# Both MLP products by three one-pass products, with the weights' parts fetched from HBM, in place of the Strassen-Winograd scheme

## The chip, the cores and the metric

The kernel runs on one core of a Trainium2 chip. The metric is the device time of one execution in microseconds (us); all times below are us unless marked ns. The result section says how ratios are computed.

## The reference

```python
kv  = einsum('bhsd,bhse->bhde', k, v)            # q, k, v: 8 x 8 x 576 x 64, fp32
out = einsum('bhsd,bhde->bhse', q, kv)
x   = out / sqrt(mean(out*out, -1) + 1e-6) * g_norm   # -> 4608 tokens x 512
h   = x @ w_in                                   # 512 x 2048
g   = h * erf(softplus(h))
y   = g @ w_out                                  # 2048 x 512
```

## The kernel before

The 4608 tokens are nine groups of 512. Group 0 multiplies in plain fp32. Groups 1 to 8 use a Strassen-Winograd scheme: seven products of half blocks in place of eight, in fp32 (four passes of TensorE), with the block sums on VectorE. The weights stay in SBUF for the whole run. The hidden features of a group are worked through in four **batches** of four 128-feature tiles; beside each batch runs a quarter of the next group's attention (two heads).

```python
def product(a, x, ps=None, first=True, last=True):          # groups 1 to 8
    ...
    for i in range(2):
        for c in range(2):
            nc.tensor.matmul(ps[:, i * H : i * H + H],      # 256 columns, fp32
                lhsT=a[:, c, i * P : i * P + P], rhs=x[:, c, :], ...)
    return ps
# --- cut: the seven hidden and seven result products of a batch, with sums ---
w_in_sb = const.tile([P, KC, DF], FP32, name="w_in_sb")     # resident weights
w_out_sb = const.tile([P, FC, DM], FP32, name="w_out_sb")
# --- cut ---
def norm():                              # the end of a quarter's attention
    ms, u, r = (st.pop(name) for name in ("ms", "u", "r"))
    nc.vector.scalar_tensor_tensor(out=u, in0=ms, scalar=EPS, in1=u, ...)   # reads PSUM
    ...
```

## Time and profile before

The median before is 1028.89 (1027.05 to 1029.86); with the run beside the changed kernel 1029.12.

| before | value | how to read it |
|---|---|---|
| TensorE (PE) busy | 1000.5, 97% of the span | the bound |
| VectorE (DVE), ScalarE (ACT) busy | 712.7, 498.5 | beside it |
| one Strassen matmul, 256 columns, fp32 | 0.2158 spacing | 112 a batch make 24.17 |
| a batch with its attention | 27.36 | a quarter of the stretch of 109.44 |
| DMA engines' busy share in that stretch | 0.15 | transfers matter nowhere after the start |

The lines that these come from stand in the prediction.

### The profile page before, as it was taken

The page shows a single profiled execution, that of the slowest core. Times are in us where ns is not written, and L with a number is a line of the kernel's source. Part 1 is how long each engine was busy: PE and PEld are TensorE (multiplying, and loading weights), DVE is VectorE, ACT ScalarE, POOL GpSimd, SP SyncE. Part 2 cuts the span into 40 slices and gives each one's busy share as a digit, 9 for nine tenths or more (in the row PEclk, how much of TensorE's full clock was granted, in tenths as well). Part 3 has the DMA queues.
Part 4 walks back from the last instruction along what each step waited for, and adds up shares of the span by engine and source line. Part 5 has one row for each costly group of instructions (what it writes and reads, how often), then busy time and mean ns, then how long its engine had stood idle before and what let it go on. Part 6 is the DMA issues. An engine that isn't in the chain of part 4 may idle for free.

```text
span 1028.0 us, 12344 instructions
## 1 busy us (share of the span) xinstructions
PE 1000.5 (97%) x4968; PEld 805.8 (78%) x4968; DVE 712.7 (69%) x1169; ACT 498.5 (48%) x654; POOL 2.4 (0%) x10
## 2 busy tenths in 40 slices
PE   6779999999999999999999999999999999999997
PEld 3334446788888888888888888888888888888886
DVE  1887895788786667657766577667865786677555
ACT  2787773444454455454444444444545544442222
POOL 0000000000000000000000000000000000000000
PEclk9999999999999999999999999999999999999999
DMA  9755511211121112001121112111200010001001
GB/s 269 203 173 159 157 42 34 78 34 37 34 77 34 37 34 74 18 22 34 49 62 34 36 34 77 34 36 34 75 1 1 1 41 1 1 1 41 1 1 42
DMA packets 67337, 55.32 MB, mean 54 GB/s; under 512 B 39632, under 2 KB 61136, under 8 KB 67280
## 3 DMA queue, kind: packets, MB, share of 16 engines
q1 hardware_dynamic: 65392, 52.24, 17.1%
q10 hardware_dynamic: 1824, 2.29, 0.8%
q8 instruction: 39, 0.64, 0.3%
q14 instruction: 18, 0.15, 0.0%
q0 software_dynamic: 64, 0.00, 0.0%
HBM read 45.09 MB, written 9.44 MB: 53 GB/s over the span
## 4 chain that ended last, share of the span: by engine, by line
PE 91%; DVE 5%; ACT 2%; DMA 1%; issue 0%; DVEq 0%
PE p_ps L521 74%; PE o_ps L370 4%; PE h_ps L445 3%; PE se_ps L292 3%; PE kv_ps L270 2%; PE qt_ps L286 2%; DMA k_sb<-in_k_dram 1%; PE ms_ps L314 1%; PE ms_ps L313 1%; DVE w_m L211 1%; DVE w_e L207 1%; DVE e L469 1%; PE kv_ps L278 1%; PE kv_ps L291 0%; DVE w_in_sb L221 0%; DVE w_out_sb L221 0%
## 5 line engine op out<-in xcount | busy, mean ns | idle before, releaser
L469 DVE TENSOR_TENSOR h_sb<-h_sb,p_ps 128x512 f32<-128x512 f32 x224 | 150.6, 684 | 160.3 <-PE p_ps L521 159.5
L393 ACT ACTIVATE s_sb<-h_sb 128x512 f32<-128x512 f32 x144 | 90.7, 630 | 312.2 <-DVE h_sb L469 311.4
L521 PE MATMUL p_ps<-w_out_sb,h_sb 128*128 128x256 f32 x768 | 176.2, 379 | 0.0
L521 PEld LDWEIGHTS p_ps<-w_out_sb,h_sb 128*128 128x128 f32 x768 | 145.9, 190 | 19.9
L521 PE MATMUL p_ps<-x_sums,a_sums 128*128 128x256 f32 x512 | 120.9, 379 | 0.0
L521 PE MATMUL p_ps<-x_sums,w_in_sb 128*128 128x256 f32 x512 | 120.9, 379 | 0.0
L521 PE MATMUL p_ps<-w_sums,s_sb 128*128 128x256 f32 x512 | 120.8, 379 | 0.0
L521 PEld LDWEIGHTS p_ps<-x_sums,a_sums 128*128 128x128 f32 x512 | 97.3, 190 | 23.9 <-issue 12.0
L469 DVE TENSOR_TENSOR e<-e,p_ps 128x512 f32<-128x512 f32 x120 | 80.7, 684 | 43.4 <-PE p_ps L521 42.2
L521 PEld LDWEIGHTS p_ps<-x_sums,w_in_sb 128*128 128x128 f32 x512 | 97.1, 190 | 14.4
L521 PEld LDWEIGHTS p_ps<-w_sums,s_sb 128*128 128x128 f32 x512 | 97.3, 190 | 13.2
L521 PE MATMUL p_ps<-xT,w_in_sb 128*128 128x256 f32 x448 | 101.3, 379 | 0.0
L521 PEld LDWEIGHTS p_ps<-xT,w_in_sb 128*128 128x128 f32 x448 | 83.2, 190 | 10.3
L100 ACT ACT_TABLE_LOAD x69 | 88.5, 1283 | 1.2
L469 DVE TENSOR_TENSOR h_sb<-h_sb,s_sb 128x512 f32<-128x512 f32 x128 | 82.2, 684 | 2.0 <-ACT s_sb L398 2.0
L398 ACT ACTIVATE s_sb<-s_sb 128x512 f32<-128x512 f32 x144 | 78.8, 618 | 0.4
L295 ACT ACTIVATE qT<-se_ps 128x512 f32<-128x512 f32 x32 | 19.1, 596 | 122.2 <-PE se_ps L292 122.2
L445 PE MATMUL h_ps<-xT,w_in_sb 128*128 128x512 f32 x128 | 61.1, 623 | 5.2 <-DVE w_in_sb L221 5.2
L521 PE MATMUL p_ps<-w_out_sb,s_sb 128*128 128x256 f32 x256 | 60.5, 379 | 0.0
L521 PE MATMUL p_ps<-w_sums,h_sb 128*128 128x256 f32 x256 | 60.5, 379 | 0.0
L370 PE MATMUL o_ps<-w_out_sb,h_sb 128*128 128x512 f32 x128 | 57.5, 593 | 0.4 <-DVE h_sb L402 0.4
L521 PEld LDWEIGHTS p_ps<-w_out_sb,s_sb 128*128 128x128 f32 x256 | 48.6, 190 | 6.6
(89 smaller groups left out, 1121.4 us busy)
## 6 DMA issues: line engine op xcount, KB each, us to landing
k_sb<-in_k_dram SPq DMA_DIRECT2D x29, 288.0 KB, 4.2
v_sb<-in_v_dram SPq DMA_DIRECT2D x29, 288.0 KB, 4.1
q_sb<-in_q_dram SPq DMA_DIRECT2D x32, 256.0 KB, 3.3
w_raw<-in_moe_w_out_dram SPq DMA_DIRECT2D x8, 1024.0 KB, 4.8
w_raw<-in_moe_w_in_dram SPq DMA_DIRECT2D x7, 1024.0 KB, 5.6
out_dram<-e SPq DMA_DIRECT2D x28, 256.0 KB, 2.1
q_last<-in_q_dram SPq DMA_DIRECT2D x16, 64.0 KB, 4.6
w_raw<-in_moe_w_in_dram SPq DMA_DIRECT2D x2, 512.0 KB, 6.3
```

Of the source, the lines that this page charges most:

```text
L100: nc.scalar.preload_act_table_set("softplus")
L207: nc.vector.scalar_tensor_tensor(out=e, in0=hi, scalar=-(1 << 31), in1=e, op0=ALU.bitwise_and, op1=ALU.bitwise_or)
L270: nc.tensor.matmul(kv_ps[s, s], lhsT=ks[:, i, c], rhs=vs[:, i, c], start=(c == 0), stop=(c == C - 1),)
L286: nc.tensor.transpose(qt_ps[:, j * P : j * P + P], qs[:, j], ident)
L292: nc.tensor.matmul(o_ps, lhsT=bd, rhs=qT, start=True, stop=True)
L295: nc.scalar.activation(qT, o_ps, AF.Square)
L370: nc.tensor.matmul(o_ps[j], lhsT=g[:, j * P : j * P + P], rhs=w_out_sb[:, f, :], start=(f == 0), stop=(f == FC - 1),)
L393: nc.scalar.activation(s, h, AF.Softplus)
L398: nc.scalar.activation(s, s, AF.Erf)
L445: nc.tensor.matmul(h_ps, lhsT=w_in_sb[:, c, n * P : n * P + P], rhs=xT[0][:, c, :], start=(c == 0), stop=(c == KC - 1),)
L469: nc.vector.tensor_tensor(out=out_, in0=x, in1=y, op=op)
L521: nc.tensor.matmul(ps[:, i * H : i * H + H], lhsT=a[:, c, i * P : i * P + P], rhs=x[:, c, :], start=(first and c == 0 and (i == 0 or last) ...
```

## The change

An fp32 number of 24 bits is cut into a high and a low part of 12 bits each, which one-pass matmuls (type fp32r) are meant to multiply exactly. Three one-pass products, of high by high, low by low, and of the two sums, replace the four passes. One product is now 12 one-pass matmuls of 512 columns: eight into `n_ps`, four into `m_ps`. The three parts of all weights (32 tiles of 786 KB, 25 MB) are not kept in SBUF: group 1, which goes back to plain fp32, cuts them and writes them to HBM, and groups 2 to 8 fetch them: four w_in tiles and four w_out tiles a batch. Three buffers hold w_in parts and seven hold w_out parts.

```diff
+    def thirds(x, high, low, both):
+        nc.scalar.activation(high, x, AF.Copy, scale=1.0 + 2.0**-13)
+        nc.vector.tensor_tensor(out=low, in0=x, in1=high.bitcast(FP32), op=ALU.subtract)
+        nc.vector.scalar_tensor_tensor(out=both, in0=low.bitcast(FP32), scalar=SHIFT, ...)
...
+        for ps, forms in ((n_ps, (0, 1)), (m_ps, (2,))):
+            for form in forms:
+                for k in range(4):
+                    nc.tensor.matmul(ps, lhsT=weights(form, k), rhs=moving(form, k), ...)
...
-    for n in range(FC):                      # group 0 in plain fp32
+    for n in range(FIRST * FC + LAG):        # groups 0 and 1 in plain fp32
...
+            h, s = hs[n], ss[n] = unit("h_sb"), unit("s_sb")
+            nc.scalar.copy(h, h_ps)
+            nc.scalar.activation(s, h, AF.Softplus)
+            if f % BATCH == BATCH - 1:
+                for i in range(n - BATCH + 1, n + 1):
+                    nc.scalar.activation(ss[i], ss[i], AF.Erf)
+                softplus_table()
+        if T == FIRST - 1:
+            for _ in range(2):
+                w_forms(*to_cut.pop(0))      # thirds() of a weight tile, store to HBM
...
+    w_in_p = ctx.enter_context(tc.tile_pool(name="w_in_p", bufs=3))
+    w_out_p = ctx.enter_context(tc.tile_pool(name="w_out_p", bufs=7, side="right"))
...
+    def hidden(T, f):
+        ps = product(...)
+        load_parts("in", 1)                  # on SyncE's queue
+        return ps
...
+        for j in range(J):
+            if old_h is not None:
+                result(T2, b2, j, g, w)
...
+        if old_h is not None:
+            load_parts("out", BATCH)         # four at once, when all results are in order
```

## The prediction

> **What bounds the kernel now.** I read the page first (busy shares, chain of waits), then the chain in order of time, then stretches of four batches.
>
> ```profile
> PE 1000.5 (97%) x4968; PEld 805.8 (78%) x4968; DVE 712.7 (69%) x1169; ACT 498.5 (48%) x654; POOL 2.4 (0%) x10
> ...
> PE 91%; DVE 5%; ACT 2%; DMA 1%; issue 0%; DVEq 0%
> ```
>
> TensorE is on the path for 91% of the span. The chain in order of time, around the change from the last group with full attention work to the one without:
>
> ```profile
> 787.58 0.85 PE kv_ps L270 x24
> 788.43 0.20 PE kv_ps L278
> 788.63 0.59 PE qt_ps L286 x4
> 789.22 8.63 PE p_ps L521 x40
> 797.86 0.17 PE kv_ps L291 x2
> 798.02 0.91 PE se_ps L292 x2
> 798.94 6.91 PE p_ps L521 x32
> 805.85 0.23 PE ms_ps L313
> 806.08 0.23 PE ms_ps L314
> 806.31 24.17 PE p_ps L521 x112
> ```
>
> A batch (a quarter of a 512-token group) holds 112 matmuls of the Strassen scheme: 24.17 us, so 0.2158 us each for 256 columns, and they stand back to back. Attention adds 0.85+0.20+0.59+0.17+0.91+0.46 = 3.2 us. Each L313/L314 (512 columns, fp32r) takes 0.23 us: a one-pass matmul of twice the columns at the same price. The stretch 296.74 to 406.18, exactly one group, confirms it:
>
> ```profile
> 296.74:406.18 109.44, 109.44 (x590) 93.93 (x589) 74.47 (x128) 51.88 (x69) 0.00 (x0) 1.00 0.15 43
> ```
>
> PE is busy in all 109.44 us, 27.36 us a batch; VectorE has 18.6 us of work a batch, ScalarE 13.0, DMA is busy 15%. The Strassen groups are purely TensorE-bound; transfers matter nowhere after the first 50 us.
>
> **What the Trainium skill says.** "FP8 and Floating Point Precision", TensorE Precision Notes: true FP32 takes four passes. The trace agrees: a 512-column fp32 matmul is two instructions of 0.43 us, the fp32r one a single 0.23. "DMA: Bandwidth & Descriptors", Measured: 341 GB/s for 1 MB, 425 for 16 MB. The trace's best full microseconds are 410 to 422:
>
> ```profile
> 113.00:114.00 1.00, 1.00 (x5) 0.47 (x3) 1.00 (x2) 0.50 (x1) 0.00 (x0) 1.00 0.99 410
> 125.00:126.00 1.00, 1.00 (x4) 0.44 (x3) 1.00 (x2) 1.00 (x1) 0.00 (x0) 1.00 1.10 242
> 126.00:127.00 1.00, 1.00 (x3) 0.38 (x2) 0.97 (x2) 0.99 (x3) 0.00 (x0) 1.00 1.03 360
> 127.00:128.00 1.00, 1.00 (x4) 0.51 (x3) 1.00 (x1) 1.00 (x2) 0.00 (x0) 1.00 0.72 210
> ```
>
> (The last two columns are the DMA engines' busy share and GB/s.) Line one is weight rows; the other three, with 0.17 of the microsecond before, are one q/k/v pair, whose small rows cost 3.0 us for 832 KB. "TensorE: Matmul & The Clock Gate", Part 1: an idle window of about 3.4 us halves the clock. The trace agrees; TensorE waited 3.44 us until 67.13 and 4.35 us until 37.41, and after the second the granted clock (third column from the right) is:
>
> ```profile
> 38.00:40.00 2.00, 2.00 (x4) 0.76 (x3) 1.97 (x4) 0.10 (x1) 0.00 (x0) 0.50 0.90 338
> 40.00:42.00 2.00, 2.00 (x5) 0.97 (x4) 1.97 (x5) 1.90 (x2) 0.00 (x0) 0.73 0.40 162
> ```
>
> "VectorE: DVE Perf Modes", tier table: fp32 tensor_tensor has no fast mode. Agrees: 0.69 us for 512 elements, 1.22 for 1024, while the one-source cast of 512 takes 0.42.
>
> **TensorE's part.** Each new product is 12 one-pass matmuls of 512 columns: 12 x 0.2158 = 2.59 us. A batch has four hidden and four result products: 20.7 us instead of 24.17, a gain of 3.45 us, in 28 batches 96.7 us. Group 1 goes back from Strassen to plain fp32: 16 x 2 x 3.43 + 12.8 of attention = 122.6 us against 109.4, a loss of 13.2. If TensorE stayed the only bound: 1029 - 83.5 = 945 us.
>
> **Group 1's extra work** is hidden: 32 cuts cost VectorE 0.69+0.69+0.42 = 1.8 us each, 57.6 of 122.6 us, beside some 33 of gates and attention; 25 MB written need 61 us at 410 GB/s.
>
> **VectorE in the new batches.** Per batch: cutting the gated values 4 x 1.22 = 4.9; hidden results 4 x 0.68 = 2.7; gates 2 x 1.22 = 2.4; result sums 8 x 0.68 = 5.5; attention with its new split 5.4. Sum 20.9 us, against 20.7 + 3.2 = 23.9 of TensorE: near, but not over. ScalarE: copies 2.3, softplus 2.5, erf 2.1, parts 2.7, attention 3.1, three table loads 3.8: 16.5.
>
> **Transfers: where I expect the gain to go.** A weight tile's three parts are 128 x 3 x 512 x 4 = 786 KB, 1.92 us at 410 GB/s. Eight a batch are 15.3 us, plus q/k/v 3.0 and the output 0.6: 19 us, under 23.9 on average. But they come in a burst and in one queue, on SyncE, which waits in program order (it stands 420 us behind transposes for q loads today). Take t = 0 as the end of a batch's last result product:
>
> 1. That product is the last reader of all four w_out tiles, so four w_out loads are issued only now: about 1.6 us until data flows (a 1 MB load issued at 103.5 lands 4.6 us later, of which 2.6 is data), then 4 x 1.92 = 7.7.
> 2. The next pair's q/k/v follow in the queue: 3.0.
> 3. w_in has three buffers, so the hidden phase starts with three tiles; the fourth is requested when the first is used up (t = 4.2) and queues behind: 1.9.
>
> It lands at 1.6+7.7+3.0+1.9+0.3 = 14.5. TensorE needs it after 1.6 (attention) + 3 x 2.59 + 1.1 (attention) = 10.5. So TensorE stands still about 4.0 us in every such batch. The loop closes: 14.5 + 2.59 + 0.47 + 4 x 2.59 = 27.9 us, no better than the 27.36 of today. In the last two groups there is no q/k/v and little attention: landing at 11.5, need at 7.8, a wait of 3.7.
>
> On the last batch of a group (its results run inside the next batch) the four output stores stand before the w_out loads in SyncE's order and wait for the last VectorE sum. VectorE is behind there: norm 2.1, two gates 2.4 and the split 1.4 lie between the sums, so that the last sum ends about 4.5 us after TensorE. That adds 5 us, with the store itself, to the next batch's wait.
>
> **The sum.** Group 0 as before; group 1's first batch starts at 152.3 in the trace; +122.6 +17.2 (five lagging projections) = 292. Stores, then first w_in tile (issued only after them): first hidden product at 297.5. Ahead of the fourth tile are ten tiles and one pair: it lands at 319.7, so the first batch ends at 322.7. The second has no w_out burst: 23.9, to 346.6. Eighteen batches of 27.9 = 502; four store delays 20; small q tails +2.5; two batches without pair loads -6: 865. Then 4 x 24.9 + 5 = 105, and 4 x 24.4 + 2 = 100: 1070. The tail (cut of the last gates with nothing beside it 5, four results 10.4, sum and store 2): 1087. A wait near 4 us can halve the clock for 3.4 us, costing up to 1.7: the trace shows it after both its waits of 3.4 and 4.4, but alignment is chance, so I count 0.5 in 27 batches, 13: 1100.
>
> **Rivals.** (a) Transfers are hidden and TensorE stays the bound: about 950 with the bubble at the change of schemes and the tail. For it: average DMA load is only 19 of 24 us, and the counts leave TensorE 96.7 us less. Against it: the queue order and three w_in buffers. (b) VectorE becomes the bound: 20.9 us plus waits behind Erf, which comes after three table loads; a period of 24.5 to 25.5, total 965 to 995. Against it: once TensorE waits for w_in, VectorE has slack. (c) The DMA rate itself is lower with writes, loads and stores mixed (0.95 busy at 269 GB/s in the first slice): at 320 GB/s the burst lands 3 us later, total near 1170.
>
> **Range and chances.** What I trust is the loop "last result, four w_out, pair, fourth w_in": one microsecond of error in it moves the total by 27. 1045 to 1140 covers two microseconds less or one and a half more. Below 1008 the wait would have to be nearly absent; I give 0.14 to having misread the order. Within 2%: 0.10.
>
> **What would show it.** Right: TensorE busy about 85%, waits before hidden products of 3 to 5 us for DMA of w_in parts, one a batch and on the fourth tile, longer after a group's end; DMA busy near 0.7; a clock below 1 in some late slices; one-pass matmuls at 0.216 us; VectorE about 21 us a batch. Wrong: a period of 24 us with no such waits (a), waits for VectorE's sums before TensorE (b), matmuls with a spacing over 0.22 us, or a fourth tile requested or delivered earlier than I read.

## More of the kernel before

A quarter of attention takes its PSUM tiles (kv_ps, qt_ps, se_ps, ms_ps) from one pool of two banks, so a new kv_ps can begin only when the norm of the quarter before has read its ms_ps.

## The result, and the profile after

The changed kernel takes **1249.62** (1243.1 to 1252.02, four runs) against 1029.12: ratio **1.2137**, 95% interval 1.2087 to 1.2186. A ratio is the mean time of one kernel's fast runs over that of the other's of the same rounds, so it is not quite the ratio of the medians quoted here. The direction was right; the time lies 150 above the prediction and 110 above the top of its range. The outputs are right.

The page of the changed kernel: busy times, the granted clock of TensorE in tenths over 40 slices, and the chain of waits by engine.

```profile
PE 1022.0 (82%) x4312; PEld 720.1 (58%) x4312; DVE 723.1 (58%) x1039; ACT 635.1 (51%) x848; POOL 2.4 (0%) x10
...
PEclk9999999888869999888988998888879998899899
...
PE 57%; DMA 20%; ACT 8%; DVE 7%; SPq 5%; issue 2%; DVEq 0%; ACTq 0%
```

TensorE is no longer the bound: a fifth of the chain is DMA. There are 656 fewer matmuls, but their busy time went up by 21.5, with a clock below full in many slices (the mean is 0.906). In e16, below, the same matmuls at a mean of 0.983 are busy 960.8. TensorE's waits, with the total, the number and the longest:

```profile
PE n_ps L413 <- DMA w_in_parts<-w_in: 145.9, 26, 11.9
PE kv_ps L274 <- DVE u L339: 29.5, 5, 7.6
PE o_ps L446 <- DVE h_sb L539: 8.4, 1, 8.4
```

The first line is the wait that the prediction named. It is 5.6 on average; in the nine batches that compare with the predicted 4.0 (with a q/k/v pair ahead, from the second new group on, not right after a group's stores) it is 4.85 to 6.56, mean 5.7. The other two it didn't have: they lie in group 1 and at its end. One batch in TensorE's order of time (start, duration, what; in brackets the idle time before and its releaser):

```profile
563.90 0.92 PE L274 MATMUL kv_ps<-v_sb,k_sb 96*64 96x64 f32 x24
...
573.79 1.10 PE L413 MATMUL m_ps<-x_forms,w_in_parts 128*128 128x512 f32 x4
580.41 3.75 PE L413 MATMUL n_ps<-x_forms,w_in_parts 128*128 128x512 f32 x8 [5.52 <-DMA w_in_parts<-w_in]
583.96 1.91 PE L413 MATMUL m_ps<-x_forms,w_in_parts 128*128 128x512 f32 x4
...
586.17 2.02 PE L413 MATMUL n_ps<-w_out_parts,g_forms 128*128 128x512 f32 x8
...
597.18 0.92 PE L274 MATMUL kv_ps<-v_sb,k_sb 96*64 96x64 f32 x24
```

Three hidden products run at once, then TensorE stands for 5.5 until the fourth w_in tile is there, 16.5 after the batch's beginning. The fourth product then takes 5.26 (580.41 to 585.67) where the others take 2.72. The stretches of 2 us around it (third column from the right is the clock, the last two are the DMA engines' busy share and GB/s) show why:

```profile
578.00:580.00 2.00, 0.00 (x0) 0.00 (x0) 1.47 (x3) 0.63 (x1) 0.00 (x0) 0.73 1.01 412
582.00:584.00 2.00, 2.00 (x7) 1.52 (x6) 0.00 (x0) 0.00 (x0) 0.00 (x0) 0.50 0.07 28
586.00:588.00 2.00, 2.00 (x10) 1.63 (x9) 0.66 (x1) 1.28 (x2) 0.00 (x0) 1.00 0.40 129
```

The clock fell to half in the wait and stayed there until the product was done. Summed over the 26 fourth products that waited for DMA, the time above 2.72 is 49.4 (from a product's start to the next matmul's, less idle time). SyncE's order of transfers in this batch:

```profile
563.32 1.96 SPq L587 DMA_DIRECT2D w_out_parts<-w_out  x4
565.62 0.62 SPq L120 DMA_DIRECT2D q_sb<-in_q_dram  x1
...
570.82 15.40 SPq L587 DMA_DIRECT2D w_in_parts<-w_in  x4
```

The order is the one that the prediction read: four w_out tiles in a burst, the q/k/v pair, then w_in. The last line joins the fourth w_in tile, issued first, with three more. Paired in this way for every batch, the time from the first w_out request to the start of the fourth product is 17.1 in the median of the thirteen batches with a pair from the second batch of the second new group on (16.4 to 18.1), 14.8 in the three batches before these, and 12.3 in the ten batches without a pair. (A batch's beginning is some 0.6 after that request, so these are 16.5, 14.2 and 11.7 on the prediction's clock. Four of the thirteen follow a group's output stores: there the request itself comes 4.3 to 4.6 after the batch's beginning, near the 5 that the prediction added for it.)

Group 1 took 180.3 (147.33 to 327.60) where the prediction has 122.6 + 17.2 = 139.8. One of its three equal waits, on TensorE, ScalarE and VectorE:

```profile
185.89 1.55 PE L274 MATMUL kv_ps<-v_sb,k_sb 96*64 96x64 f32 x24 [7.64 <-DVE u L339]
```
```profile
177.41 2.19 ACT L555 ACTIVATE s_sb<-s_sb 128x512 f32<-128x512 f32 x4
179.62 1.28 ACT L103 ACT_TABLE_LOAD   x1
180.91 0.63 ACT L376 ACTIVATE w_new<-w_in_sb 128x512 fp32r<-128x512 f32 x1
```
```profile
181.58 0.69 DVE L377 TENSOR_TENSOR w_new<-w_in_sb,w_new 128x512 fp32r<-128x512 f32 x1 [7.99 <-ACT w_new L376]
...
185.16 0.68 DVE L339 SCALAR_TENSOR_TENSOR u<-ms_ps,u 128x512 f32<-128x512 f32 x1
```

Read backwards: TensorE's next kv_ps waits for the norm (L339) to free its bank; the norm stands behind the weights' cut in VectorE's program order; the cut waited 7.99 for its high part; and that copy stands behind four Erf and two table loads in ScalarE's order. VectorE was idle meanwhile.

### The profile page after: what moved, and what is told of

It reads as the page before. It is cut to its first block, busy times and chain, and to the rows that moved or that the text cites. A ratio compares the mean times of both kernels' runs of the same rounds, so it can differ in the third digit from the quotient of the medians.

```text
span 1250.2 us, 11817 instructions
## 1 busy us (share of the span) xinstructions
PE 1022.0 (82%) x4312; PEld 720.1 (58%) x4312; DVE 723.1 (58%) x1039; ACT 635.1 (51%) x848; POOL 2.4 (0%) x10
## 4 chain that ended last, share of the span: by engine, by line
PE 57%; DMA 20%; ACT 8%; DVE 7%; SPq 5%; issue 2%; DVEq 0%; ACTq 0%
PE n_ps L413 25%; DMA w_in_parts<-w_in 16%; PE m_ps L413 12%; PE h_ps L543 8%; PE o_ps L446 7%; SPq L125 4%; DMA w_out_parts<-w_out 4%; PE kv_ps L274 2%; PE qt_ps L296 1%; PE se_ps L302 1%; ACT L103 1%; DVE h L396 1%; DMA q_last<-in_q_dram 1%; ACT L100 1%; DVE e L396 1%
## 5 line engine op out<-in xcount | busy, mean ns | idle before, releaser
L413 PE MATMUL n_ps<-x_forms,w_in_parts 128*128 128x512 f32 x896 | 275.8, 457 | 154.1 <-DMA w_in_parts<-w_in 145.9
L413 PEld LDWEIGHTS n_ps<-x_forms,w_in_parts 128*128 128x128 f32 x896 | 189.1, 216 | 215.6 <-issue 149.0
L413 PE MATMUL n_ps<-w_out_parts,g_forms 128*128 128x512 f32 x896 | 226.2, 395 | 9.8 <-ACT e L391 7.1
L413 PEld LDWEIGHTS n_ps<-w_out_parts,g_forms 128*128 128x128 f32 x896 | 170.3, 191 | 48.9 <-ACT e L391 9.3
L396 DVE SCALAR_TENSOR_TENSOR h<-m_ps,h 128x512 f32<-128x512 f32 x112 | 77.1, 688 | 208.9 <-PE m_ps L413 167.5
L413 PE MATMUL m_ps<-x_forms,w_in_parts 128*128 128x512 f32 x448 | 135.2, 428 | 0.0
L396 DVE SCALAR_TENSOR_TENSOR e<-m_ps,e 128x512 f32<-128x512 f32 x112 | 76.7, 690 | 75.9 <-ACT e L391 61.9
L413 PE MATMUL m_ps<-w_out_parts,g_forms 128*128 128x512 f32 x448 | 120.2, 390 | 0.0
L413 PEld LDWEIGHTS m_ps<-x_forms,w_in_parts 128*128 128x128 f32 x448 | 96.0, 214 | 23.6
L413 PEld LDWEIGHTS m_ps<-w_out_parts,g_forms 128*128 128x128 f32 x448 | 84.7, 189 | 17.9
L376 ACT ACTIVATE g_forms<-h 128x1024 fp32r<-128x1024 f32 x56 | 59.0, 1053 | 17.0 <-DVE h L670 15.7
L670 DVE TENSOR_TENSOR h<-h,s 128x1024 f32<-128x1024 f32 x56 | 65.8, 1217 | 0.2 <-ACT s L657 0.2
L274 PE MATMUL kv_ps<-v_sb,k_sb 96*64 96x64 f32 x768 | 33.2, 243 | 39.3 <-DVE u L339 29.5
```

The costliest lines, as they stand in the source:

```text
L274: nc.tensor.matmul(kv_ps[s, s], lhsT=ks[:, i, c], rhs=vs[:, i, c], start=(c == 0), stop=(c == C - 1),)
L376: nc.scalar.activation(high, x, AF.Copy, scale=1.0 + 2.0**-13)
L396: nc.vector.scalar_tensor_tensor(out=out_, in0=ps, scalar=scale, in1=out_, op0=ALU.mult, op1=ALU.add)
L413: nc.tensor.matmul(ps, lhsT=weights(form, k), rhs=moving(form, k), start=(form == forms[0] and k == 0), stop=(form == forms[-1] and k == 3),)
L670: nc.vector.tensor_tensor(out=h[:, part], in0=h[:, part], in1=s[:, part], op=ALU.mult)
```

## The experiments

My theories after reading the traces: (1) the late fourth tile, through the burst of w_out loads and the pair ahead of it; (2) group 1's order of work; (3) the half clock after each wait; and beneath these (4) VectorE's and ScalarE's chain, the prediction's rival (b). The rival to (1) was that the rate of the transfers is too low, whatever their order. Each run is an edit of the changed kernel unless said otherwise.

### e1_cut_early: group 1's weight cuts ahead of the softplus

```diff
+        if T == FIRST - 1:
+            for _ in range(2):
+                w_forms(*to_cut.pop(0))
         if T < FIRST:
             h_ps = ps_h.tile(...)       # the block stood behind Erf and its table loads
```

> Only the place of the weight cuts in group 1 changes: they come before the copy and softplus of the same step, so ScalarE's part of a cut no longer stands behind the four Erf and the table loads. Theory: the three waits of 7.64 us before the attention products and the one of 8.44 us before the projections, with the half clock after each, are due to this order; they vanish, the second group's stretch (147 to 328 us) shrinks by 35 to 42 us, total about 1212. Rival: VectorE or the stage buffers are the limit, the waits only move: total 1240 or more.

Measured: 1224.49, ratio 1.1899 (1.1867 to 1.193), so 25 less. Group 1 shrank from 180.3 to 153.8 (146.95 to 300.78): the three waits of 7.64 became 1.48, and the one of 8.44 became 2.90. The cause is confirmed, the size was overestimated; 14 over the predicted 139.8 remain: 8.8 of TensorE's waits and, at a mean clock of 0.967, about 5 of lost clock.

### e2_one_by_one: no burst of w_out loads

```diff
                 ps = hidden(T, b * BATCH + i)
+            if m > first_batch + 1:
+                load_parts("out", 1)
...
-        if old_h is not None:
-            load_parts("out", BATCH)
```

> The four w_out loads of a batch are no longer issued together after the last result, but one after each hidden product of the next batch, each behind the w_in load. Theory (the burst ahead of the fourth w_in tile is the wait): with at most the q/k/v pair ahead, the fourth tile is there in time, the period falls from about 33 to 25 or 26 us (8 products of 2.72 and 3.2 of attention), the clock returns to 1.0 in the last three quarters, total 1030 to 1060. Rival (VectorE is the next bound, 21 us of work with waits behind Erf): period 27 to 29, total 1090 to 1140. Rival (DMA cannot sustain it): waits for w_in stay, total over 1180.

Measured: 1132.4, ratio 1.1002 (1.0985 to 1.1018), 117 less. The waits for w_in fell from 145.9 to 23.0 (10 waits), with the same bytes at the same queue; so it is the order, not the average rate. The total is not the theory's 1030 to 1060 but in the range of the second rival, VectorE as the next bound. In their place came `ms_ps <- DVE sq_hi`, 32.1 in 19 waits: theory 4 showed itself.

### e3_fill: keep TensorE busy in the wait

Twenty spare one-pass matmuls run into the product's own PSUM bank (and are overwritten) before each fourth hidden product.

```diff
+        if fill is not None:
+            for _ in range(20):
+                nc.tensor.matmul(n_ps, lhsT=fill[:, 0:P], rhs=fill, start=True, stop=True)
```

> Twenty spare one-pass matmuls (4.5 us at 0.227) stand before the fourth hidden product, so that TensorE works while it would wait. The arrival of the tile does not change. Theory (the halved clock after the wait costs about 2.5 us a batch): the fourth hidden product takes 2.8 instead of 5.3 us, the clock stays near 1.0 except after the long waits, total 1250 - 20 to 26 times 2.5 = 1185 to 1200. Rival (that product is slow for another reason, such as the transfers beside it): 1250 or more.

Measured: 1235.31, ratio 1.2009 (1.1986 to 1.2032), only 14 less. The fourth product of the same batch now ran at full clock, though it started 16.6 after its batch's beginning, as late as before:

```profile
586.19 2.12 PE L416 MATMUL n_ps<-x_forms,w_in_parts 128*128 128x512 f32 x8 [1.10 <-DMA w_in_parts<-w_in]
```

PE was busy 1108.7, of which 560 x 0.2267 = 127 is the fill; the remaining 981.7 is 40 less than 1022.0 for the same work. So the half clock cost at least 40 there (49.4 by the count above). The sum closes: waits for w_in 145.9 - 46.8 = 99 less, work 40 less, fill 127 more, which is 12 less; 14 were measured. Filling the gaps buys the clock, not the time.

### e4_pairs_late: the q/k/v pair behind the fourth tile

```diff
-            load_pair(T * NP + p + 2)
+            if T <= FIRST:
+                load_pair(T * NP + p + 2)
...
                 ps = hidden(T, b * BATCH + i)
+                if i == 0:
+                    load_pair((T + 1) * NP + b + 2)
```

> Only the q/k/v loads of a pair move: behind the request of the fourth w_in tile instead of ahead of it. The burst of w_out stays. By bytes in one queue the tile lands 3.0 us earlier (t0 + 13.5 instead of 16.5). Theory 1 (strictly first in, first out by bytes, the rest of the delay is elsewhere): wait of about 2.5 us stays, period 30 to 31, total 1190 to 1215. Theory 2 (the pair also unbalances the 16 DMA engines, which costs the other 2 us): t0 + 11.5, hardly a wait, no half clock, period 26 to 27, total 1110 to 1150.

Measured: 1194.19, ratio 1.159 (1.1551 to 1.163). The waits for w_in fell to 95.9 (25). From the first w_out request to the fourth product it is now 14.7 in the median of the same thirteen batches, where it was 17.1, and 11.9 in the three before them, where it was 14.8. Theory 1 holds. But in batches without a pair it is 12.2, so the thirteen are 2.5 later even with the pair behind; e15 comes back to this.

### e5_loads_once: no transfers of weights at all in the new groups

The buffers are loaded once and used again, which gives a wrong result.

```diff
+                if len(had) < bufs:
+                    t = pool.tile([P, 3, G], FP32, ...)
+                    nc.sync.dma_start(out=t, in_=w_kept[key])
+                else:
+                    t = had[len(had) % bufs]
```

> Wrong results on purpose: the first three w_in and seven w_out tiles are loaded once and used for all batches, so no weights are fetched in the batches; the rest is as in the changed kernel (the cuts of group 1 too). It shows the bound without transfers. If TensorE is it: 8 products of 2.72 and 3.2 of attention, period 25.0 us, total 1025 to 1040, clock 1.0 after the second group. If the chain through ScalarE and VectorE is it (the fp32 halves that the mean waits for stand behind the cuts): period 27 to 28, total 1070 to 1095. It also tells whether the hidden products' 2.85 us fall to 2.72 with no loads beside them.

Measured: 1111.56, ratio 1.0809 (1.0783 to 1.0835). Transfers cost 138 of the 221 that the change lost. The total is above both of my ranges. Without any, a group takes 112.7, or 28.2 a batch, still more than the 27.36 of before. The reason is a wait that the transfers had covered:

```profile
PE ms_ps L323 <- DVE sq_hi L315: 44.0, 23, 4.4
```

VectorE isn't short of time (65% busy). In a batch it stands 1.65 for ScalarE's high part of the gated values and 1.54 for ScalarE's copy of a product, both of which stand behind other work in ScalarE's order; its next instruction, the split of the squares, then comes late for TensorE.

### e6_own_queue: w_in loads from GpSimd

```diff
-                nc.sync.dma_start(out=t, in_=w_kept[key])
+                side = nc.gpsimd if which == "in" else nc.sync
+                side.dma_start(out=t, in_=w_kept[key])
```

> The w_in loads go to the idle GpSimd's DMA queue, the w_out burst and the pair stay on SyncE's. If the tile is late because it stands behind the burst in one queue: it lands by t0 + 11 to 12 (request at 4.4, about 1.5 to data, twice 1.92 for sharing the engines, a little more), hardly a wait, total 1100 to 1150. If all traffic shares the 16 engines such that a tile lands only when most of the rest has: t0 + 15 to 17 as before, total 1230 to 1260.

Measured: 1130.64, ratio 1.0987 (1.0955 to 1.102). A queue of its own gives as much as undoing the burst, but keeps a wait of about 2.2 in nearly every batch (56.5 in 26).

### e7_one_two: e1 and e2 together

> The early cuts of the first experiment and the one-by-one w_out loads of the second together. They act on different stretches (before and after 330 us), so the gains should add: 1250 - 25 - 117 = 1108, within 5 us. If the loads or stores of the cuts matter to the later part, it differs by more than 10.

Measured: 1103.97, ratio 1.0727 (1.07 to 1.0755). The two add: 25 + 117 = 142 from 1249.6 would be 1107.5.

### e8_all: e7 with w_in on GpSimd's queue, and both high parts first

In `cut`, ScalarE's two copies of the high parts are ordered ahead of the products' copies.

> The two together, w_in on its own queue, and ScalarE's two copies for the cuts of the gates both ahead of the hidden copies (VectorE stood idle 1.65 us a batch for the second). If the remaining waits are the fourth tile (23 us in all) and the halves of the squares (32 us): 1108 - 20 - 30 - up to 10 of half clock = 1045 to 1065. If VectorE and ScalarE stay the bound: 1090 or more.

Measured: 1114.28, ratio 1.0844 (1.0809 to 1.0878), worse than e7. The waits for the split of squares fell to 1.5, but waits for w_in were back (56.7 in 21): GpSimd's queue loses once w_out no longer comes in a burst. Two edits in one run hid that one was good, as e9 indicates, which has it together with a later softplus.

### e9_act_order: e7 with ScalarE's order alone changed

```diff
+            if old_h is not None and i == 0:
+                cuts = [cut(old_h, half) for half in range(2)]   # both high parts first
...
-                nc.scalar.activation(s[:, i], h[:, i], AF.Softplus)
+                if i:
+                    nc.scalar.activation(s[:, i - 1], h[:, i - 1], AF.Softplus)
```

> On top of the two repairs (1104 us): ScalarE's order alone changes, both copies for the gates' cuts first and each softplus one hidden product later. Without any transfer the batch took 28.2 us, with VectorE idle twice, 1.65 and 1.54 us, for a ScalarE copy that stood behind a softplus. Theory (this chain, not VectorE's 21 us of work, holds the mean's matmuls up): both gaps go, the waits for the fp32 halves (30 us in all) go, period 25.3 to 26, total 1030 to 1060. Rival (VectorE is simply full): 1090 or more.

Measured: 1051.63, ratio 1.0218 (1.0184 to 1.0252), 52 less than e7. VectorE's and ScalarE's busy times are as before (718.9 and 635.5); only the order changed. This settles theory 4.

### e10_changeover: e9, and the first loads of the new groups earlier

The first three w_in loads come before the last five lagging projections of group 1, and w_out loads one by one from the first new batch.

> On top of that: the first three w_in loads are issued before the last five projections instead of after the stores, and the seven w_out loads at the change of schemes come one by one. The waits there (6 us for the first tile, 13 us for the fourth, with the half clock after each) should go: 18 to 22 us less, total 1010 to 1040. It is also the attempt to beat the kernel before, 1029.

Measured: 1028.29, ratio 1.0008 (0.9994 to 1.0022): level with the kernel before, and within the expectation.

### e11_pitch: the price of a one-pass matmul

Three lots of 16 spare matmuls before each fourth product: fp32r of 256 columns, bf16 of 512, fp32r of 512.

> Before each fourth hidden product 48 spare matmuls from tiles in place: 16 one-pass fp32r of 256 columns, 16 bf16 of 512, 16 one-pass fp32r of 512. Only their spacing counts. If a one-pass fp32r matmul costs a fixed 11 ns more than 512 columns of a four-pass one: 0.120 us for 256, 0.227 for 512. If it streams columns 5% slower: 0.113 and 0.227. If 512 columns in one instruction cost that in any type: 0.227 for bf16 too, else 0.216.

Measured spacings at full clock: 0.119, 0.2157 and 0.2267. The whole series in one batch:

```profile
592.64 9.20 PE L415 MATMUL n_ps<-x_forms 128*128 128x256 f32 x48
601.68 1.56 PE L419 MATMUL n_ps<-x_forms,w_in_parts 128*128 128x512 f32 x6
```

From start to start these are 9.04, and 16 x (0.119 + 0.2157 + 0.2267) = 8.98. A bf16 matmul of 512 columns costs what a Strassen matmul of 256 did; an fp32r one costs 11 ns more at 512, and 0.119 at 256 is about 10 ns over the bf16 spacing there, by an estimate from the Trainium skill's formula (256/2.4 + 2.5 = 109 ns; "TensorE: Matmul & The Clock Gate", section "Wait — 56ns, not 53.3ns?"). So it looks like a fixed extra, not a rate: 5% on that estimate would be 5 ns. A bf16 matmul of 256 columns was not measured.

### e12_requests_late and e13_behind_fourth: two edits that changed nothing

Both meant to keep younger w_in requests from sharing the DMA engines with the fourth tile, by ordering `load_parts("in", ...)` as 1, 0, 0, 3 over the four products; e13 also asked for the last of the three first.

> In the changed kernel only the w_in requests behind the fourth tile's move: all three are issued after the fourth hidden product. Burst and pair stay ahead. If loads issued later share the engines with the fourth tile and so delay its landing (by bytes in turn it should land at t0 + 14.4, it lands at 16.5): 2 us earlier in each batch, total 1190 to 1215. If it is imbalance between the 16 DMA engines: no change, 1240 to 1255.

> The twelfth run changed nothing in SyncE's stream: requests wait only for their buffers, so the two w_in loads after the fourth were still issued at once. Now the load into the fourth tile's own buffer, which must wait for the fourth hidden product, stands first, so nothing is issued behind the fourth tile before it has landed. Burst and pair stay ahead. If later loads share the engines with it: it lands at about t0 + 14.4 instead of 16.5, in the last two groups (no pair) at about 11.5 instead of 13.7; total 1185 to 1215. If not (imbalance of the engines, a slower rate): 16.5 and 13.7 as before, total 1240 to 1260.

Measured: 1251.57 and 1253.01, ratios 1.2165 (1.2145 to 1.2186) and 1.2157 (1.2127 to 1.2187). SyncE's requests were where they had been. In these runs a request waited only for its buffer and for the requests before it on SyncE; moving it later among the instructions of the other engines did not delay it. In e13 the fourth tile's request went out at 572.77, and two younger ones still at 573.26 and 576.63, before the fourth product. These runs tell nothing of the sharing.

### e14_more_repairs: e10 with three further edits

The first sums of a group's results on VectorE instead of ScalarE, output stores on GpSimd's queue, and the weights' cuts of group 1 ahead of the attention pieces.

> On top of the version that ties with the kernel before (1028): the first result sums of a group on VectorE instead of ScalarE (waits of 8.6 us), output stores of the new batches on GpSimd's queue so that SyncE does not stand behind VectorE's last sum (part of 15.3 us of waits for w_in), and the cuts of group 1 ahead of the attention pieces of their step (11.0 us). If these waits are on the path: 1028 - 20 to 30 = 998 to 1010, 2 to 3% under the kernel before. If other waits take their place: 1018 to 1028.

Measured: 1034.45, ratio 1.0054 (1.0038 to 1.007), worse than e10. Waits for ScalarE's sums were gone (8.6 to 0), those for w_in fell from 15.3 to 9.8; but `kv_ps <- DVE u` was back at 29.5 in 5 waits, the same as in the changed kernel. The third edit had put the norm behind the cuts again, and the cuts behind the Erf of the step before.

### e15_hold_requests: nothing behind the fourth tile

The changed kernel with a 2 KB transfer that reads the fourth hidden result between the fourth tile's request and the next three.

```diff
+                if i == BATCH - 1:
+                    nc.sync.dma_start(out=held, in_=h[0:1, i])
+                    load_parts("in", 3)
```

> The changed kernel with one tiny transfer (2 KB) on SyncE that reads the fourth hidden result and stands between the fourth tile's request and the next three w_in requests, so that nothing at all is issued behind the fourth tile until its product has been evicted (e12 and e13 meant to do this, and the trace showed that they left SyncE's requests where they were). If the fourth tile is late because younger transfers share the engines with it: it lands about 14.4 us after the batch's first request in batches with a pair of q/k/v loads and 11.5 in the last groups, the waits on w_in shrink by about 2 us a batch, total 1185 to 1215. If it is late for another reason (a transfer's own end costs, the sum of older transfers): 16.5 and 13.7 as before, total 1240 to 1260. It could also lose a little at the other end: the next batch's three tiles come later, but there is a whole batch for them.

Measured: 1248.58, ratio 1.2112 (1.2085 to 1.2139): no change beyond the spread. SyncE's order and TensorE's fourth product in the same batch as above:

```profile
563.88 1.96 SPq L587 DMA_DIRECT2D w_out_parts<-w_out  x4
...
571.20 0.40 SPq L587 DMA_DIRECT2D w_in_parts<-w_in  x1
586.66 0.24 SPq L654 DMA_DIRECT2D held<-h  x1
```
```profile
580.37 3.75 PE L413 MATMUL n_ps<-x_forms,w_in_parts 128*128 128x512 f32 x8 [4.92 <-DMA w_in_parts<-w_in]
```

The hold works, and the tile is as late as before: from the first w_out request to the fourth product 16.9 in the median of the thirteen batches (17.1 before) and 12.2 in the ten without a pair (12.3 before). Younger w_in loads cost at most 0.2, and the theory that the fourth tile shares the engines with them falls, with a pair and without. (The 13.7 that my expectation gives for the last groups was a misreading; paired with their requests, those batches of the changed kernel have 12.3.) The stretches, first three of this batch, then three of a batch of the last groups (no q/k/v pair), show what is:

```profile
577.00:578.00 1.00, 0.00 (x0) 0.00 (x0) 0.00 (x0) 1.00 (x3) 0.00 (x0) 1.00 1.00 333
578.00:579.00 1.00, 0.00 (x0) 0.00 (x0) 0.69 (x2) 0.28 (x1) 0.00 (x0) 1.00 0.19 68
579.00:580.00 1.00, 0.00 (x0) 0.00 (x0) 0.97 (x3) 0.63 (x1) 0.00 (x0) 0.70 0.04 18
1186.00:1187.00 1.00, 0.00 (x0) 0.00 (x0) 0.00 (x0) 1.00 (x2) 0.00 (x0) 1.00 1.01 424
1187.00:1188.00 1.00, 0.00 (x0) 0.00 (x0) 0.69 (x1) 0.24 (x2) 0.00 (x0) 1.00 0.74 307
1188.00:1189.00 1.00, 0.38 (x2) 0.36 (x3) 0.00 (x0) 0.48 (x1) 0.00 (x0) 1.00 0.00 0
```

With a pair in the queue all 16 DMA engines are busy until 578.2; then a busy share that falls from 0.28 to 0.09 and less, at 12 to 37 GB/s, about one engine of sixteen, goes on until some 580.0, and the product starts at 580.37. The batch after it shows the same: a share of 0.06 from 611.5 to 613.0, product at 613.66. Without a pair the share drops from full to nothing within half a microsecond. "DMA: Bandwidth & Descriptors" of the skill, section "Why a DMA increments its semaphore by 16 and not by 1", says that a transfer runs on up to 16 engines that finish independently, and counts as done when all have. The trace agrees: the tile is late by the engine that is last, 1.8 here. The rest of the pair's price is its rate: from 573 to 578 the engines are full at only some 320 GB/s, against 418 to 430 in the no-pair batch from 1182 to 1187.

In the three batches before the thirteen there is a pair but no such tail (the share drops from 0.43 to 0 at 445.0), and there a pair costs 14.8 - 12.2 = 2.6 rather than 4.7. The DMA view of e15's batch (`--dma --window 560:590`) has a line that may say why:

```profile
q8 instruction: 1, 0.02, 0.2%
```

It is one packet of 16 KB on a queue that brings instructions; it starts at 572.31 and takes one DMA engine 0.99. In the changed kernel, take the batches with a pair that do not follow a group's stores. In the nine where a packet of an instruction queue (16 or 8 KB) starts between the first w_out request, or 0.1 before it, and the fourth product, this time is 16.4 to 18.0; in the three where none does, 14.7 to 15.7. In e15 it is 16.5 to 17.8 against 14.8 to 15.3, and in e4, with the pair behind, 13.4 to 15.3 against 11.8 to 12.4. With neither pair nor packet it is 11.6 to 12.1 in the changed kernel. So a pair ahead may cost only the predicted 3.0, and a pair behind nothing, the other 2 or so going with one engine that an instruction packet has held up. The three are always the first three batches, but in e15 two later batches without such a packet (requests at 495.76 and 633.77) have a tail of only 0.4 and 0.5. No run moved these packets, so this is a coincidence in three traces and not shown as the cause.

### e16_two_repairs: e10 with two of the three edits of e14

```diff
-            for step in in_full(es[j], ps):
-                step()
+            nc.vector.tensor_scalar(out=es[j], in0=ps[0], scalar1=1.0 - 1.0 / SHIFT, ...)
+            add_scaled(es[j], ps[1], 1.0 / SHIFT)
...
-            nc.sync.dma_start(out=rows[:, j, :], in_=e)
+            (nc.gpsimd if T >= FIRST else nc.sync).dma_start(out=rows[:, j, :], in_=e)
```

> e10 with two of the three edits of e14: the first sums of a group's results on VectorE in place of ScalarE (waits of 8.6 us in e10 that e14 showed gone) and the output stores of the new batches on GpSimd's queue; without e14's third edit, which put the norm behind the weights' cuts again. Theory (the parts add): 1028 less 8.6, less some 5 of waits on w_in, less up to 4 in group 1: 1008 to 1016, ratio about 0.983 to 0.99. Rival (VectorE, which gets the sums, becomes late elsewhere, or the wait moves to the next landing): 1022 to 1030, a tie.

Measured: **1009.37** (1002.62 to 1013.99), ratio **0.98** (0.9769 to 0.9831): faster than both kernels, though the record's verdict at a limit of 2% is "unclear", because the interval holds 0.98. The time is within the expectation (1008 to 1016). The page, and a stretch of 100 us inside the new groups:

```profile
PE 960.8 (95%) x4312; PEld 680.3 (67%) x4312; DVE 739.5 (73%) x1067; ACT 621.0 (62%) x820; POOL 15.5 (2%) x34
...
PE 78%; DMA 7%; DVE 7%; ACT 5%; issue 1%; SPq 1%; DVEq 0%
```
```profile
500.00:600.00 100.00, 98.29 (x514) 78.45 (x513) 77.59 (x113) 63.27 (x83) 2.17 (x4) 1.00 0.80 298
```

In this stretch TensorE is the bound again, at full clock (over the whole span the mean is 0.983), with the same products and the same 257 MB of transfers. A batch takes 25.6 here (four from 500.16 to 602.53), against 27.36 before.

## Why the prediction was wrong

The direction, the mechanism (a late fourth w_in tile in nearly every batch, put there by the burst, the pair and three buffers) and the sequence of requests were right. The sum was short by 150. Along the trace, by the prediction's own stages:

| stage | predicted | measured | more |
|---|---|---|---|
| start to group 1's first batch | 152.3 | 147.3 | -5 |
| group 1 with the lagging projections | 139.8 | 180.3 | +40 |
| to the first hidden product of the new scheme | 5.5 | 6.8 | +1 |
| its first two batches | 25.2 + 23.9 | 65.8 | +17 |
| eighteen batches | 502 + 20 + 2.5 - 6 | 603.9 | +85 |
| eight batches of the last groups | 105 + 100 | 227.9 | +23 |
| last results and store | 17 | 18.2 | +1 |
| half clock, counted apart | 13 | in the stages | -13 |

- **"Group 1's extra work is hidden"** failed: +40. I compared amounts (57.6 of VectorE in 122.6) and didn't follow the order on each engine. The amount was indeed hidden; the place in the order was not. e1 takes back 25 by order alone. The same wait (5.07 before a kv_ps at 369.48) and a half-clock stretch behind it are part of the +17.
- **"It lands at 1.6+7.7+3.0+1.9+0.3 = 14.5"** was a term mis-sized, and only where a pair is ahead. On the prediction's clock it was 16.5 in thirteen batches (+2.0, 26 in all; in the four after stores, counted from their later request), 14.2 in the three before them, and 11.7 without a pair, where 11.5 was predicted. In e15's batch the terms can be read one by one, counted from the request: full rate after 1.6, as predicted; 7.5 at about 400 GB/s, predicted 7.7 for w_out; 5.2 for the pair and the tile, predicted 3.0 + 1.9; bytes done after 14.3. The missing term is the last engine's 1.8 (what held that engine up stays open; e15 has a lead), and the start 0.4 after it, where I had 0.3.
- **"A wait near 4 us can halve the clock ... I count 0.5 in 27 batches"** was a term mis-sized: 13 counted, 49.4 measured, of which 34 lie in the eighteen batches and 13 in the last eight. Of these 26 products 23 took 4.2 to 5.26 instead of 2.72. I took alignment for a chance that would save most of them; it saved few. It does play a part:

```profile
1015.15 3.20 PE L413 MATMUL n_ps<-x_forms,w_in_parts 128*128 128x512 f32 x8 [2.25 <-DMA w_in_parts<-w_in]
1191.70 2.08 PE L413 MATMUL n_ps<-x_forms,w_in_parts 128*128 128x512 f32 x8 [3.46 <-DMA w_in_parts<-w_in]
```

After the wait of 2.25 the clock was at half from 1015.8 to 1019.2 and the product took 4.42; after the longer wait of 3.46 it stayed full, and the product took 2.85.
- **"12 x 0.2158 = 2.59"** was a term mis-sized: 0.2267, read across from another kind of matmul, though the prediction's own lines show L313 and L314 at 0.23 each, which it took for "the same price". The matmuls that are on the path in a batch (four result products and the fourth hidden one, 60) make 60 x 0.0109 = 0.65, or 18 in 28 batches (e11). The prediction's own check ("a spacing over 0.22 us") went against it.

In the eighteen batches 26 + 34 + 12 = 72 of the 85 are named; in the last eight 13 of clock, 5 of pitch and 2 of landing are 20 of the 23. The remaining 13 and 3 lie in waits that I didn't take apart (for ScalarE's first sums 7.1 in all, for one).

**The rivals.** (a) was refused by 145.9 of waits. (c), a lower DMA rate, is refused by e2, which moves the same bytes 117 faster, and by the 400 GB/s of the burst; the pair's 320 GB/s cost 0.3 (5.2 where 3.0 + 1.9 was predicted). (b) I set aside because TensorE's wait would give VectorE slack. That holds while the tile is late, but e5 shows (b) underneath at nearly the same height: 28.2 a batch without any transfer, beside the 27.9 that was predicted with them. It is not VectorE's amount of work, of which the prediction's 24.5 to 25.5 was made, but its waits for ScalarE (e9: 52 for two changes of order).

**Where the expected gain was.** Part of the gain of TensorE that the prediction had worked out is there: e16 gets a batch from 27.36 to 25.6, where the prediction's products and attention alone would take 23.9, and 25.0 at the measured 2.72 a product. From the changed kernel to e16, 146 came back through e1 and e2 together, 52 through ScalarE's order, 23 at the changeover and 19 through the sums and stores: 240. None takes away work; each changes an order, an engine or a queue.

## What to carry to other kernels

Adding up an engine's work tells whether it can be hidden; only its program order, followed instruction by instruction to the one that another engine waits for, tells whether it is. When a resident operand becomes a fetched one, ask the loads one by one as their buffers come free, and price a wait of TensorE with the half-clock stretch behind it: here 1.9 us on average over 26 waits, and a wait of 2.25 us was enough. Try repairs one at a time: e8 and e14 each hid a good edit under a bad one.

## What the Trainium skill lacked or had wrong

- **The price of an fp32r matmul.** "TensorE: Matmul & The Clock Gate" gives N/2.4 + 2.5 ns, which fits bf16 here (0.2157 for 512 columns), but it has no line on fp32r: 0.2267 for 512, 11 ns more, and 0.119 for 256, about 10 ns more by the estimate above (e11, 18 us in this kernel).
- **What a wait costs through the clock.** The same page, section "HAM oscillation — how this bites in real kernels", describes waits of 3 to 5 us with a stretch of about 1.67 us at half clock behind each. The trace agrees in kind and is worse in size: 26 products behind waits took 49.4 more, or 1.9 each, which is 3.8 at half clock; behind waits of 5 us and more the product took 4.6 to 5.3 instead of 2.72.
- **How long a wait halves the clock.** The same page, Part 1, which the prediction cites, has an idle window of about 3.4 us. Here a wait of 2.25 was enough (before 1015.15) and one of 3.46 was not (before 1191.70).
- **A lagging DMA engine.** "DMA: Bandwidth & Descriptors" says that the engines finish independently, but I found no number there for what small rows do to a large transfer behind them, or for one engine that lags: here batches with a pair of 832 KB are 4.8 later (17.1 against 12.3), of which about 1.8 is a tail on about one engine (e15) that may come from an instruction packet (not shown).
- **Younger transfers on the same queue.** I found no number on that page for what they cost an older one. Here, with two loads of 786 KB issued while the older one was on its way (571.70 and 574.92 in the batch above), at most 0.2 (e15).
